# A turn more in front of TensorE's loop in an attention decode kernel on one Trainium2 core

## The chip, the cores and the metric

The kernel runs on one core of one Trainium2 chip. The metric is the device time of one execution in microseconds (us). The kernel before takes 184.91 us, the median of three runs (184.82 to 184.98).

## The reference, cut to what matters

One new token for each of 32 sequences attends to the last 512 cached positions. There are 32 query heads, and four of them share one of 8 key and value heads.

```python
B, Sq, D = x.shape                      # 32, 1, 512
Hq, Dh = 32, 128
Hkv, Sk = k_cache.shape[1], k_cache.shape[2]   # 8, 2048
W = min(4096, max(256, Sk // 4))        # 512
rep = Hq // Hkv                         # 4
q = (lambda x, *d: x.transpose(*d))((x @ wq).reshape(B, Sq, Hq, Dh), 0, 2, 1, 3)
k = jnp.repeat(k_cache[:, :, Sk - W:, :], rep, axis=1)
v = jnp.repeat(v_cache[:, :, Sk - W:, :], rep, axis=1)
scores = jnp.einsum("bhqd,bhkd->bhqk", q, k) * (Dh ** -0.5)
p = _softmax(scores, axis=-1)
o = jnp.einsum("bhqk,bhkd->bhqd", p, v)
return (lambda x, *d: x.transpose(*d))(o, 0, 2, 1, 3).reshape(B, Sq, Hq * Dh) @ wo
```

All inputs are bf16. The window of keys is 32 x 8 x 512 x 128 x 2 bytes, 33.6 MB, the values are as many, and wq and wo have 4.2 MB each.

## The kernel before

The 32 sequences are taken as eight **quads** of four, numbered 0 to 7. For one quad the keys are 4 MiB and the values 4 MiB, and each has two buffers in SBUF (`K_sb`, `V_sb`); even quads use one, odd quads the other. The buffer of wq is later a buffer of values, and that of the even keys later holds wo.

Every engine works through a list of short words, written out by hand at the top of the file (lines 20 to 37). The letter is an operation, the first number its quad:

- **T q.w** (VectorE, line 522) transposes half of the quad's keys, w being 0 or 1.
- **S q.w** (TensorE, `scores`, line 353) does half of the quad's scores, 16 matmuls.
- **M q** (VectorE, line 528) takes the row maximum, **X q** (ScalarE, line 581) the exponential with its sum, **N q** (VectorE, line 536) divides by the sum.
- **E q** (TensorE, `to_value_rows`, line 366) regroups the probabilities to the rows of the values, 16 matmuls; **G q** (ScalarE, line 588) takes them out of PSUM, and **B q.a.b** (VectorE line 542 and ScalarE line 594, heads a to b) spreads them into a block-diagonal form.
- **P q.a.b** (TensorE, `pv`, line 378) multiplies by the values, four matmuls for each step from a to b of 32.
- **C q.a.b** and **I** take the results out of PSUM, **F q** (TensorE, `fold`, line 390) folds them, **D q** (ScalarE, line 606) stores them for the output projection (line 464).

SyncE issues all large loads in one order (`LOADS`, lines 34 to 37): two halves of wq, then K0 K1 V0 K2 K3 V1 K4 V2 K5 and so on, the last values in halves, and wo in three parts W0, W1, W2. Its queue is in order. Loads of keys from K2 on wait for the second transpose of the quad two before (line 246), so K3 waits for T1.1 and K4 for T2.1; loads of values from V2 on wait for P of the quad two before (line 253). V1 overwrites wq and waits for the projection of the queries (line 250).

TensorE projects the queries first. Then come six operations written out as straight code, `PE_HEAD` (line 20): S0.0 S0.1 S1.0 S1.1 E0 E1. Then a hardware loop on TensorE alone (line 436) makes four turns; each turn does two rounds of `PE_ROUND` (line 21). Round q is S(q+2).0, P q.0.16, F(q-1), S(q+2).1, P q.16.28, E(q+2), P q.28.32. In the last turn there are no quads 8 and 9, so S, E and the second round's F stand under `pe.If(turn < NQ - 2)`. There are six such blocks in a turn. After the loop follow F6, F7 and the output projection, as straight code.

VectorE and ScalarE run straight code in the orders of lines 24 to 32. VectorE begins T0.0 T0.1 T1.0 M0 T1.1 N0 M1 N1 B0.0.4 T2.0 T2.1, and ScalarE X0 G0 X1 G1 B0.4.8 B1.4.8 X2 G2. T q.w waits for S(q-1).w, whose operand it overwrites; N1 waits for E0, which reads the same buffer `P_bf`; G and X follow their E and M. GpSimd builds the block-diagonal queries of quad q (line 316) once S(q-2).1 is done.

TensorE waits for semaphores in `awaited` (line 399 on). In the loop the value waited for is worked out in a register from the turn (`looped`, line 439), and held in a register for the rest of the turn. The semaphore for C counts both engines that take results out; a memset on GpSimd (line 295) gives it a start value of 4, so that the loop's first round, whose F stands for a quad -1, has something to find.

Of the kernel before, what the change touches and what calls it, by code (L numbers as in the profile page):

```python
# [2 lines left out]

# [13 lines left out]

PE_HEAD = "S0.0 S0.1 S1.0 S1.1 E0 E1"  # L20
PE_ROUND = "S{3}.0 P{1}.0.16 F{0} S{3}.1 P{1}.16.28 E{3} P{1}.28.32"
PE_TAIL = "F6 F7"
ROUNDS = 8
# [19 lines left out]
def ops_of(text):  # L43
    return [(w[0],) + tuple(int(n) for n in w[1:].split(".")) for w in text.split()]


def bass_standalone__sliding_block_cached__sampling_kernel(
# [7 lines left out]
):  # L55
    B, Sq, D = x.shape
    _, HKV, SK, DH = k_cache.shape
    HD = wq.shape[1]
    HQ = HD // DH
# [6 lines left out]
    NQ = B // 4  # L66
# [2 lines left out]
    NI = 32  # L69
    NG = 4  # L70

    rounds = [PE_ROUND.format(q - 1, q, q + 1, q + 2) for q in range(ROUNDS)]
    real = lambda w: int(w[1:].split(".")[0]) < NQ and w != f"F{NQ - 2}"
    rounds = [" ".join(w for w in r.split() if real(w)) for r in rounds]
    orders = {
        "PE": ops_of(" ".join([PE_HEAD] + rounds + [PE_TAIL])),
        "DVE": ops_of(DVE_OPS), "ACT": ops_of(ACT_OPS),
    }

    def counter(eng, op):  # L80

        if op[0] == "T":
            return ("DVE", "T%d" % op[2]), 1
        if op[0] == "C":
            return ("both", "C"), op[3] - op[2]
        if op[0] == "I":
            return ("both", "I%d" % op[3]), 1
        return (eng, op[0]), 1

    ends, total = {}, {("ACT", "D"): 2, ("both", "C"): 4}  # L90
    for eng, ops in orders.items():
        for op in ops:
            kind = op[0]
            key, n = counter(eng, op)
            total[key] = total.get(key, 0) + n
            if kind in "BP":
                for i in range(op[2], op[3]):
                    ends[kind, op[1], i] = key + (total[key],)
            elif kind == "C":
                for i in range(op[2], op[3]):  # L100
                    ends[kind, op[1], i] = key + (4 * op[1] + 8,)
            elif kind != "I":
                ends[op] = key + (total[key],)

# [23 lines left out]
    with ExitStack() as es:  # L128
# [14 lines left out]
        C_sb = sb("C_sb", [P, 2, 4, DH], F32)  # L143
# [52 lines left out]
        s = {n: sem(n) for n in names}  # L196
        op_sem = {key: sem("op_%s_%s" % key) for key in total}
# [20 lines left out]
        def single(eng):  # L218

            once = eng.alloc_register("once")  # L220
            eng.reg_mov(once, 1)
            return nc.Fori(0, once, 1, engines=[eng.engine], hint_back_edge=True)
# [48 lines left out]
        @block.gpsimd  # L271
        def _(pool):
            with single(pool):
                wait = Waits(pool)

                def diag(t, pattern, name):
                    pool.memset(t, 0.0).then_inc(s[name], 1)
                    pool.wait_ge(s[name], 1)
                    pool.affine_select(
                        out=t, in_=t, compare_op=ALU.not_equal, fill=1.0,  # L280
                        base=0, pattern=pattern, channel_multiplier=1,
                    ).then_inc(s[name], 1)

                diag(xsel[:, :, :], [[-1, 4], [-4, 32]], "pool_x")
                pool.memset(junk[:, 0:2], 0.0).then_inc(s["pool_j"], 1)
                pool.memset(QBD[:, :, :, :], 0.0).then_inc(s["pool_q"], 1)
                diag(F_id[:, :, :], [[-32, 4], [-1, HQ]], "pool_f")
                diag(m_id[:, :, :, :], [[-32, 4], [-4, HKV], [-1, KB]], "pool_m")
                pool.memset(F_sb[:, :, :, :], 0.0).then_inc(s["pool_fz"], 1)
                whole = [w for w in ops_of(" ".join(LOADS)) if w[0] == "V" and w[2:] == (0, R)]  # L290
                pool.memset(junk[:, 2:3], 0.0).then_inc(
                    sem_v_end[0], 16 * sum(w[1] % 2 == 0 for w in whole))
                pool.memset(junk[:, 3:4], 0.0).then_inc(
                    sem_v_end[1], 16 * sum(w[1] % 2 for w in whole))
                pool.memset(C_sb[:, 1], 0.0).then_inc(op_sem["both", "C"], 4)

                diag(E_id[:, :, :].rearrange("p e (b h) -> p e b h", b=4),
                     [[-1, REP], [-4, 4], [-16, HKV]], "pool_ei")
                pool.memset(E_sb[:, :, :, :, :], 0.0).then_inc(s["pool_e"], 1)
                pool.wait_ge(s["pool_e"], 1)  # L300
                pool.wait_ge(s["pool_ei"], 2)
                for k in range(KB):
                    pool.tensor_copy(E_sb[:, k, :, :, k], E_id[:, :, :]).then_inc(s["pool_e"], 1)
                pool.wait_ge(s["pool_e"], 5)
                pool.wait_ge(s["pool_q"], 1)
                pool.wait_ge(s["dve_QT"], 1)
                for q in range(NQ):
                    if q >= 2:
                        wait([ends["S", q - 2, 1]])
                    for b in range(4):  # L310
                        pr = slice(32 * b, 32 * b + 32)
                        if b:
                            pool.wait_ge(s["pool_qbd"], 3 * q + b)
                        elif q:
                            pool.wait_ge(s["pool_quad"], q)
                        pool.tensor_copy(  # L316
                            QBD[pr, q % 2].rearrange("p (w t) (h c) -> p w t h c", w=2, h=HKV)[
                                :, :, :, :, 4 * b:4 * b + 4],
                            QT_sb[pr, q].rearrange("p w (h e) t -> p w t h e", h=HKV),
                        ).then_inc(s["pool_quad" if b == 3 else "pool_qbd"], 1)  # L320

        @block.tensor
        def _(pe):
# [75 lines left out]
            def awaited(op):  # L399

                kind = op[0]
                if kind == "S":
                    yield op_sem["DVE", "T%d" % op[2]], 1, 1
                    if op[2] == 0:
                        yield s["pool_quad"], 1, 1
                        yield op_sem["both", "C"], 4, -4
                elif kind == "E":
                    yield op_sem["DVE", "N"], 1, 1
                elif kind == "P":
                    if op[2] == 0:  # L410
                        yield op_sem["DVE", "B"], 1, 1
                        yield op_sem["ACT", "B"], 1, 1
                        yield op_sem["ACT", "D"], 1, 1
                        yield op_sem["ACT", "G"], 1, 2
                        yield sem_v[op[1] % 2], 8, 16 - 8 * (op[1] % 2)
                    elif op[2] == 16:
                        yield sem_v_end[op[1] % 2], 8, 16 - 8 * (op[1] % 2)
                elif kind == "F" and op[1] < NQ - 1:
                    yield op_sem["both", "C"], 4, 8

            def do(op, value):
                for sm, a, b in awaited(op):
                    if (v := value(op[1], a, b)) is not None:
                        pe.wait_ge(sm, v)
                run[op[0]](*op[1:]).then_inc(op_sem["PE", op[0]], 1)
# [4 lines left out]
            pe.wait_ge(s["dve_q"], 4)  # L430
            pe.wait_ge(s["act_q"], 4)
            pe.wait_ge(s["dve_c"], 7)
            for op in ops_of(PE_HEAD):
                if op == ("E", 0):
                    pe.wait_ge(s["pool_e"], 5)
                do(op, plain)
            with nc.Fori(0, ROUNDS, 2, engines=[mybir.EngineType.PE]) as turn:
                held = {}

                def looped(q, a, b):  # L440
                    key = (skipped, a, a * q + b)
                    if key not in held:
                        v = turn * a + (a * q + b)
                        held[key] = pe.snap(v & 7 if key == (False, 1, 3) else v)
                    return held[key]

                for p in range(2):
                    words = PE_ROUND.format(p - 1, p, p + 1, p + 2).split()
                    for skipped, group in groupby(words, lambda w: w[0] in "SE" or p == 1 and w[0] == "F"):
                        with pe.If(turn < NQ - 2) if skipped else nullcontext():  # L450
                            for op in ops_of(" ".join(group)):
                                do(op, looped)
            for op in ops_of(PE_TAIL):
                do(op, plain)
# [196 lines left out]
```

## Time and profile before

| what | value |
|---|---|
| median of three runs | 184.91 us |
| the profiled execution | 184.95 us |
| its span, first to last instruction | 183.1 us |
| around the span | 1.85 us |
| TensorE busy | 118.9 us (65%), 1644 matmuls and as many weight loads |
| VectorE busy | 102.7 us (56%) |
| ScalarE busy | 53.0 us (29%) |
| GpSimd busy | 17.5 us (10%) |
| mean granted TensorE clock | 0.83 of full speed |
| read from memory | 75.53 MB, 413 GB/s over the span |
| issue to landing, keys, 4096 KB | median 22.7 us |
| issue to landing, values, 4096 KB | median 26.4 us |

The profile shows one execution. All times in it are counted from the start of the span. PE is TensorE, PEld its weight loads, DVE VectorE, ACT ScalarE, POOL GpSimd, SP SyncE; L378 is line 378 of the kernel. A load of 4096 KB at the 413 GB/s of the span takes about 10 us alone; that it lands 22.7 or 26.4 us after its issue says that others stand in the queue before it. Sixteen DMA engines share each load, and a load has landed when the last of them is done with its part.

### The profile page before, as it was taken

How to read it: one execution, taken by the hardware profiler on the slowest of the kernel's cores; microseconds unless marked ns; L12 is line 12 of the kernel's file. 1: busy time of each engine (PE TensorE's matmuls, PEld its weight loads, DVE VectorE, ACT ScalarE, POOL GpSimd, SP SyncE). 2: the span in 40 equal slices, each digit the busy share in tenths (PEclk: the TensorE clock that was granted, in tenths of full speed). 3: DMA queues.
4: the chain of work that ended last, by engine and by line, in shares of the span. 5: the costliest groups of instructions: out<-in, count | busy, mean ns of one | idle time of the engine just before them, and what ended most of it. 6: DMA issues, size and time to landing. Idle time of an engine off the chain costs nothing.

```text
span 183.1 us, 3778 instructions
## 1 busy us (share of the span) xinstructions
PE 118.9 (65%) x1644; PEld 55.4 (30%) x1644; DVE 102.7 (56%) x103; ACT 53.0 (29%) x100; POOL 17.5 (10%) x55
## 2 busy tenths in 40 slices
PE   0089204446203996896289945994599499999772
PEld 0024001003201353353035402541145154454362
DVE  0030999995339729949921895059905993503031
ACT  3000400010590015624700390028302832812041
POOL 7910050202000020020000100020000000000000
PEclk9999855555855699999859965699589999999998
DMA  6999999899999999899999999999989999999980
GB/s 219 418 465 401 451 458 444 387 429 458 454 401 401 458 454 422 383 451 454 437 401 422 458 444 408 408 458 444 444 372 444 408 451 408 444 415 437 420 363 26
DMA packets 3572, 75.63 MB, mean 413 GB/s; under 512 B 432, under 2 KB 496, under 8 KB 624
## 3 DMA queue, kind: packets, MB, share of 16 engines
q1 hardware_dynamic: 3504, 75.53, 96.6%
q8 instruction: 4, 0.07, 0.1%
q10 hardware_dynamic: 64, 0.03, 0.1%
HBM read 75.53 MB, written 0.03 MB: 413 GB/s over the span
## 4 chain that ended last, share of the span: by engine, by line
DMA 52%; PE 32%; DVE 11%; ACT 1%; SPq 1%; ACTq 1%; issue 1%; DVEq 0%
DMA V_sb<-in_v_cache_dram 26%; PE ps L378 19%; DMA K_sb<-in_wo_dram 12%; DMA K_sb<-in_k_cache_dram 11%; DVE KT_sb L522 7%; PE ps L340 4%; DMA bd<-in_x_dram 4%; PE ps L353 4%; PE ps L390 2%; PE ps L366 2%; DVE QT_sb L514 2%; DVE KT_sb L511 1%; ACT C_sb L599 1%; ACTq L200 1%; SPq L260 1%
## 5 line engine op out<-in xcount | busy, mean ns | idle before, releaser
L378 PE MATMUL ps<-V_sb,bd 32*128 32x512 bf16 x1024 | 66.9, 411 | 9.7 <-DMA V_sb<-in_v_cache_dram 9.6
L522 DVE STREAM_TRANSPOSE KT_sb<-K_sb 128x4096 f32<-128x4096 f32 x16 | 70.1, 4421 | 4.2 <-DMA K_sb<-in_k_cache_dram 4.1
L353 PE MATMUL ps<-KT_sb,QBD 128*32 128x512 bf16 x256 | 22.7, 485 | 38.3 <-DVE KT_sb L522 25.8
L378 PEld LDWEIGHTS ps<-V_sb,bd 32*128 32x128 bf16 x1024 | 27.0, 100 | 47.5 <-issue 18.6
L528 DVE TENSOR_REDUCE maxv<-ps 128x1 f32<-128x512 f32 x8 | 5.5, 687 | 30.1 <-PE ps L353 30.1
L353 PEld LDWEIGHTS ps<-KT_sb,QBD 128*32 128x32 bf16 x256 | 6.1, 107 | 50.6 <-issue 22.4
L594 ACT ACTIVATE bd<-PTc,mask 128x512 bf16<-128x512 bf16 x32 | 20.3, 710 | 0.2
L316 POOL COPY QBD<-QT_sb 32x128 bf16<-32x128 bf16 x32 | 9.2, 287 | 102.7 <-PE ps L353 86.4
L581 ACT ACTIVATE P_f<-ps,negmax 128x512 f32<-128x512 f32 x8 | 5.5, 686 | 39.0 <-DVE negmax L530 39.0
L599 ACT ACTIVATE C_sb<-ps 32x512 f32<-32x512 f32 x24 | 14.1, 587 | 5.9 <-PE ps L378 5.7
L606 ACT ACTIVATE o_sel<-ps 128x128 bf16<-128x128 f32 x8 | 2.2, 277 | 34.1 <-PE ps L390 34.1
L588 ACT ACTIVATE PTc<-ps 128x512 bf16<-128x512 f32 x8 | 4.8, 597 | 20.9 <-PE ps L366 20.9
L390 PE MATMUL ps<-C_sb,F_sb 128*128 128x128 f32 x72 | 10.6, 290 | 0.2 <-DVE C_sb L551 0.2
L366 PE MATMUL ps<-P_bf,E_sb 128*128 128x128 bf16 x128 | 9.1, 228 | 2.1 <-DVE P_bf L536 2.1
L390 PEld LDWEIGHTS ps<-C_sb,F_sb 128*128 128x128 f32 x72 | 8.8, 191 | 3.9 <-issue 3.4
L340 PE MATMUL ps<-V_sb,bd 128*128 128x512 bf16 x32 | 9.3, 462 | 0.8 <-DVE bd L490 0.8
L366 PEld LDWEIGHTS ps<-P_bf,E_sb 128*128 128x128 bf16 x128 | 7.7, 102 | 5.6 <-DVE P_bf L536 4.8
L542 DVE TENSOR_SCALAR bd<-PTc,mask 128x512 bf16<-128x512 bf16 x32 | 8.9, 343 | 0.0
L547 DVE COPY C_sb<-ps 32x512 f32<-32x512 f32 x4 | 2.8, 693 | 8.1 <-PE ps L378 8.1
L328 PE MATMUL ps<-bd 32*128 32x128 bf16 x4 | 0.6, 296 | 9.0 <-DMA bd<-in_x_dram 9.0
L511 DVE CAST KT_sb<-ps 128x512 bf16<-128x512 f32 x4 | 2.5, 684 | 6.7 <-PE ps L340 6.7
L575 ACT ACTIVATE KT_sb<-ps 128x512 bf16<-128x512 f32 x4 | 2.1, 603 | 14.3 <-PE ps L340 14.3
(34 smaller groups left out, 36.6 us busy)
## 6 DMA issues: line engine op xcount, KB each, us to landing
K_sb<-in_k_cache_dram SPq DMA_DIRECT2D x8, 4096.0 KB, 22.7
V_sb<-in_v_cache_dram SPq DMA_DIRECT2D x5, 4096.0 KB, 26.4
V_sb<-in_v_cache_dram SPq DMA_DIRECT2D x6, 2048.0 KB, 18.3
V_sb<-in_wq_dram SPq DMA_DIRECT2D x2, 2048.0 KB, 9.8
K_sb<-in_wo_dram SPq DMA_DIRECT2D x1, 2048.0 KB, 17.6
K_sb<-in_wo_dram SPq DMA_DIRECT2D x1, 1536.0 KB, 20.7
K_sb<-in_wo_dram SPq DMA_DIRECT2D x1, 512.0 KB, 21.4
out_dram<-P_bf SPq DMA_DIRECT2D x1, 32.0 KB, 1.5
```

The costliest lines, as they stand in the source:

```text
L316: pool.tensor_copy(QBD[pr, q % 2].rearrange("p (w t) (h c) -> p w t h c", w=2, h=HKV)[:, :, :, :, 4 * b:4 * b + 4], QT_sb[pr, q].rearrange ...
L340: ins = pe.matmul(ps[:, n], lhsT=xT_sb[:, kt, :], rhs=wq_sb[:, kt, n * 512:(n + 1) * 512], start=kt == 0, stop=kt == DKT - 1, tile_positio ...
L353: ins = pe.matmul(s_bank(q)[32 * c:32 * c + 32, :], lhsT=QBD[:, q % 2, 2 * w + t, c0:c0 + 32], rhs=KT_sb[:, w, :, KB * h:KB * h + KB, t], ...
L366: ins = pe.matmul(e_bank(q)[:, e * R:(e + 1) * R], lhsT=E_sb[:, k, e].rearrange("p m j -> p (m j)"), rhs=P_bf[:, k * R:(k + 1) * R], start ...
L378: ins = pe.matmul(o_banks(q)[:, b, :], lhsT=bd[pr, q % 2, 4 * g:4 * g + 4].rearrange("p r h e -> p (r h e)"), rhs=V_sb[q % 2][pr, 512 * g: ...
L390: ins = pe.matmul(f_bank(q)[:, 0:P], lhsT=F_sb[:, d].rearrange("p h d -> p (h d)"), rhs=C_sb[:, q % 2, :, 32 * d:32 * d + 32], start=d == ...
L522: return dve.transpose(KT_sb[:, w].bitcast(F32).rearrange("p r c t -> p r (c t)"), K_sb[q % 2][:, :].bitcast(F32).rearrange("p (r w c) -> ...
L528: dve.tensor_reduce(maxv[:, q:q + 1], s_bank(q), AX.X, ALU.max).then_inc(s["dve_m"], 1)
L542: ins = dve.tensor_scalar(o, i, m, None, op0=ALU.mult)
L581: return act.activation(P_f32[:, :].rearrange("p (k r) -> p k r", k=KB), s_bank(q).rearrange("p (r k) -> p k r", k=KB), ACTF.Exp, bias=neg ...
L594: ins = act.activation(o, i, ACTF.Copy, scale=m)
L599: ins = act.activation(*pick_args(q, r), ACTF.Copy)
```

## The change

`PE_HEAD` and the code that it made are gone. The loop makes five turns instead of four; the new first turn stands for rounds -2 and -1. Of these only S0.0, S0.1, E0 and S1.0, S1.1, E1 are real. So the order of the six becomes S0.0 S0.1 E0 S1.0 S1.1 E1, that of a round.

Every operation of the loop now stands under an `If`, in one of three kinds: S and E run while `turn < 8`, P and the first round's F while `late < 8`, the second round's F while `late < 6`. `late` is the turn less 2, wrapped to 14 in the first turn. There are 13 such blocks in a turn in place of six. Values waited for in the first kind are worked out from the turn, in the two others from `late`. The start value of the semaphore for C becomes 12, with all that wait for it raised by 8, so that S0.0 and S1.0 find 4 and 8. The wait for the constants of E (`pool_e`), which stood before E0, stands before the loop.

```diff
-PE_HEAD = "S0.0 S0.1 S1.0 S1.1 E0 E1"
 PE_ROUND = "S{3}.0 P{1}.0.16 F{0} S{3}.1 P{1}.16.28 E{3} P{1}.28.32"
...
-    rounds = [PE_ROUND.format(q - 1, q, q + 1, q + 2) for q in range(ROUNDS)]
-    real = lambda w: int(w[1:].split(".")[0]) < NQ and w != f"F{NQ - 2}"
+    rounds = [PE_ROUND.format(q - 1, q, q + 1, q + 2) for q in range(-2, ROUNDS)]
+    real = lambda w: -(w[0] == "F") <= int(w[1:].split(".")[0]) < NQ and w != f"F{NQ - 2}"
...
-        "PE": ops_of(" ".join([PE_HEAD] + rounds + [PE_TAIL])),
+        "PE": ops_of(" ".join(rounds + [PE_TAIL])),
...
-    ends, total = {}, {("ACT", "D"): 2, ("both", "C"): 4}
+    ends, total = {}, {("ACT", "D"): 2, ("both", "C"): 12}
...
-                    ends[kind, op[1], i] = key + (4 * op[1] + 8,)
+                    ends[kind, op[1], i] = key + (4 * op[1] + 16,)
...
-                pool.memset(C_sb[:, 1], 0.0).then_inc(op_sem["both", "C"], 4)
+                pool.memset(C_sb[:, 1], 0.0).then_inc(op_sem["both", "C"], 12)
...
-                        yield op_sem["both", "C"], 4, -4
+                        yield op_sem["both", "C"], 4, 4
...
-                    yield op_sem["both", "C"], 4, 8
+                    yield op_sem["both", "C"], 4, 16
...
-            for op in ops_of(PE_HEAD):
-                if op == ("E", 0):
-                    pe.wait_ge(s["pool_e"], 5)
-                do(op, plain)
-            with nc.Fori(0, ROUNDS, 2, engines=[mybir.EngineType.PE]) as turn:
+            pe.wait_ge(s["pool_e"], 5)
+            with nc.Fori(0, ROUNDS + 2, 2, engines=[mybir.EngineType.PE]) as turn:
+
+                late = pe.snap((turn + 14) & 15)
                 held = {}
 
-                def looped(q, a, b):
-                    key = (skipped, a, a * q + b)
-                    if key not in held:
-                        v = turn * a + (a * q + b)
-                        held[key] = pe.snap(v & 7 if key == (False, 1, 3) else v)
-                    return held[key]
+                def group_of(p, w):
+                    return "keys" if w[0] in "SE" else "fold" if p == 1 and w[0] == "F" else "values"
 
                 for p in range(2):
                     words = PE_ROUND.format(p - 1, p, p + 1, p + 2).split()
-                    for skipped, group in groupby(words, lambda w: w[0] in "SE" or p == 1 and w[0] == "F"):
-                        with pe.If(turn < NQ - 2) if skipped else nullcontext():
-                            for op in ops_of(" ".join(group)):
+                    for group, ws in groupby(words, lambda w: group_of(p, w)):
+
+                        def looped(q, a, b):
+                            key = (group, a, a * q + b)
+                            if key not in held:
+                                if group == "keys":
+                                    v = turn * a + (a * q + b - 2 * a)
+                                else:
+                                    v = late * a + (a * q + b)
+                                held[key] = pe.snap(v & 7 if key == ("values", 1, 3) else v)
+                            return held[key]
+
+                        runs = {"keys": turn < NQ, "values": late < NQ, "fold": late < NQ - 2}
+                        with pe.If(runs[group]):
+                            for op in ops_of(" ".join(ws)):
                                 do(op, looped)
```

## The prediction

> **What bounds the kernel now.** I read the page's summary first, then the chain that ended last, then the DMA records, and then the stretch around the six moved operations engine by engine.
>
> ```profile
> span 183.1 us, 3778 instructions
> ...
> DMA  6999999899999999899999999999989999999980
> ...
> q1 hardware_dynamic: 3504, 75.53, 96.6%
> q8 instruction: 4, 0.07, 0.1%
> ```
>
> The loads (queue q1) fill 96.6% of the span on all 16 DMA engines; no slice is lower than 8 tenths but the first and the last. TensorE and VectorE sit idle a third and more of it. So the kernel is a stream of 75.5 MB, and an engine's delay counts only if a load is issued so late that the stream runs dry. The chain in order of time says the same:
>
> ```profile
> 33.11 20.03 DMA K_sb<-in_k_cache_dram
> 53.15 0.02 issue
> 53.17 4.46 DVE KT_sb L522
> ...
> 158.67 21.42 DMA K_sb<-in_wo_dram
> 180.09 0.04 issue
> 180.14 0.42 PE ps L464 x15
> ```
>
> K2 lands at 53.15 and VectorE waits for it; at the end W2 lands at 180.09, and only then come the last 16 matmuls and the output.
>
> The second row of the queues is the one to look at in this change: four packets of queue q8, 65,536 bytes in all, are the program's own code. I followed the single packets of the trace. On one DMA engine a packet begins within 4 ns of the end of the one before, so the sixteen engines can be told apart. The code packets run at 47.5, 68.4, 77.8 and 85.5 us, each on one engine for 1.02 to 1.09 us; that engine's loads stand still meanwhile (holes of 1.00 to 1.07 us), and its next packet takes 1.69 to 1.76 us in place of 1.21. Together about 1.5 us. None runs after 86 us. At the end, from 176 us in 40 slices of 0.175 us:
>
> ```profile
> DMA  9839699899431222231100000000000000150000
> ```
>
> Most engines are done at 178, and a quarter or an eighth is busy until 179.5. By the packets, twelve deliver their last data at 177.8 to 178.2 us, and four at 179.24, 179.29, 179.62 and 179.64: those are the four that fetched code. As W2 has landed only when all 16 are done, **the code packets set the end of the stream**.
>
> Now the six operations, TensorE and VectorE:
>
> ```profile
> 33.14 1.90 PE L353 MATMUL ps<-KT_sb,QBD 128*32 128x512 bf16 x16 [2.23 <-DVE KT_sb L522]
> 37.47 1.90 PE L353 MATMUL ps<-KT_sb,QBD 128*32 128x512 bf16 x16 [2.43 <-DVE KT_sb L522]
> 42.58 1.90 PE L353 MATMUL ps<-KT_sb,QBD 128*32 128x512 bf16 x16 [3.22 <-DVE KT_sb L522]
> 44.41 1.58 PE L366 MATMUL ps<-P_bf,E_sb 128*128 128x128 bf16 x16
> 48.07 1.13 PE L366 MATMUL ps<-P_bf,E_sb 128*128 128x128 bf16 x16 [2.08 <-DVE P_bf L536]
> 57.75 1.90 PE L353 MATMUL ps<-KT_sb,QBD 128*32 128x512 bf16 x16 [8.55 <-DVE KT_sb L522]
> ```
>
> ```profile
> 42.61 0.48 DVE L536 TENSOR_SCALAR P_bf<-P_f,recip 128x512 bf16<-128x512 f32 x1
> 44.53 0.69 DVE L528 TENSOR_REDUCE maxv<-ps 128x1 f32<-128x512 f32 x1 [1.44 <-PE ps L353]
> 47.93 1.14 DVE L542 TENSOR_SCALAR bd<-PTc,mask 128x512 bf16<-128x512 bf16 x4
> 53.17 8.77 DVE L522 STREAM_TRANSPOSE KT_sb<-K_sb 128x4096 f32<-128x4096 f32 x2 [4.10 <-DMA K_sb<-in_k_cache_dram]
> ```
>
> These are S0.1, S1.0, S1.1, E0, E1, S2.0; and N0, M1, B0.0.4, T2.0. The last line has the cover: 4.10 us in which VectorE waits for K2.
>
> **The change part by part.**
>
> *The order.* E0 now stands ahead of S1.0, and waits for N0, which ends at 42.61 + 0.48 = 43.09. Behind it on TensorE wait S1.0 and S1.1, whose operands are ready at 37.4 and 42.5. E0 takes 1.58 us, S1.0 and S1.1 1.90 each: 43.1 + 5.4 = 48.5. M1 begins there in place of 44.53, **4.0 us later**. X1 no longer stands behind G0, so M1's begin to N1's end is what later rounds show (66.80 to 69.22, 2.42 us): N1 ends at 51.0, B0.0.4 at 52.1. T2.0 can't begin before K2 is there at 53.17. So VectorE's 4.10 us of idle time shrink to about 1.0, and T2.0, T2.1 and the issue of K4 stay. ScalarE: E1 51.1 to 52.7, G1 0.6, four spreads 2.6 (half of 4.99 for eight), so B0.4.8 is there at 55.9; P0 wants it at 59.58. GpSimd's queries for quad 3 follow S1.1 at 49.9 (four copies, 1.33), wanted by S3.0 at 73.9. Price 0.
>
> *If that cover is gone*, the stream's backlog stands behind it. When K4 is issued at 61.97, 28,672 KB have been issued (wq, K0 to K3, V0, V1), 29.36 MB. Moved by then: 18 us at 428 GB/s, 20 at 419, 20 at 443 and 2 at 419, 25.8 MB. The rest of 3.6 MB lasts 8.6 us. A load's first packet comes 1.0 us after its issue (0.73 to 1.76 at the start), so K4 may come 7.5 us later without a gap, and M1's chain 8.5 us.
>
> *The blocks under `If`*, 13 in place of 6 a turn, and a fourth way back to the loop's head. The nearest row is where P5.28.32 and P6.0.16 follow each other across a way back and a skipped block:
>
> ```profile
> 155.90 4.77 PE L378 MATMUL ps<-V_sb,bd 32*128 32x512 bf16 x80
> ...
> 161.69 3.63 PE L378 MATMUL ps<-V_sb,bd 32*128 32x512 bf16 x64
> ```
>
> The 64 matmuls of P6.16.32 take 3.63 us with a skipped block among them, so 80 would take 4.54: 0.23 us for the way back with its skipped block, 0 for the other. Bounds 0 to 0.23 for each; I take 0, as the row with a block alone has it. At 0.23 the eight blocks of the first turn between E0 and E1 cost 1.8 us, inside the 8.5. In later rounds P waits 2.0 to 3.6 us for its values (quads 2 to 4), and seven more blocks a turn at 0.23 are 0.8 us a round. At the end the last turn's groups lie ahead of V6 and V7, for which P waits 0.20 and 1.16 us, and W2 is the later one anyway.
>
> A rule that speaks against the change stands in the Trainium skill, "Runtime: NRT & Kernel Launch", section "Instruction fetch mechanics": a taken branch to code outside the window of two blocks waits for that block to be fetched. By it each way back over the loop would fetch again. The trace disagrees for TensorE's loop here: turns after the first fetch nothing, nor do the ways back at 125 and 157 us. If the rule holds in the first turn, it is the stall of the fourth rival.
>
> *The code.* 96 of 644 pairs of weight load and matmul leave the program (from the code: 4 + 32 + 96 + 368 + 16 + 128). When the packets ran, TensorE had come to about pair 116, 266, 383 and 500: one packet for some 128 new pairs. The new program has 548, with its loop at 36 to 404, and skips through it in the first turn. So I expect **three packets instead of four**, between 30 and 55 us. The first may hold up K1, which T1.0 takes up at 33.1; by the windows' rates K1 lands near 32, and 1.5 us more make T1.0 up to 0.5 us late, inside the 1.0.
>
> What does a packet less bring? Three engines late by 1.5 us still end the stream as four do. Bounds: the ends of 179.62 and 179.64 belong to two engines that without a packet would have been among the later of the twelve, those of 179.24 and 179.29 to two earlier ones. With three packets on the same engines as the first three, one of 179.62 stays: -0.02. If all three fall on early ones, 179.64 - 179.29 = 0.35 less; with the lateness at its spread, -0.40 to +0.07. I take -0.02, as the second and fourth packets sit on the late pair and only the fourth goes.
>
> *Other edits:* the `pool_e` wait is met at 9.7 us, when GpSimd's fourth copy for E ends, long before 29; the memset's larger count is the same instruction. Waits on register values in the first turn are as in S2.0, which begins 0.13 us after T2.0 ends. All 0.
>
> **Sum:** 184.95 + 0 + 0 - 0.02 = 184.93 for an execution like the profiled one, which lies 0.04 above the median: **184.89 us**.
>
> **The rivals.**
>
> 1. *The three packets fall on early engines.* W2 lands 0.33 to 0.40 us sooner: 184.91 - 0.33 = 184.58, to 184.51. For it: which engine gets which packet is not in the profile. Against: two of four sat on late ones.
> 2. *No code packet in the stream's way*, if all code is there before the loads fill the queue. The twelve other engines end at 178.2, but then TensorE bounds: from 177.22 the output matmuls need 1.08 + 0.85 + 0.43, ending at 179.6 in place of 180.57. 184.91 - 1.0 = 183.9. Against it: new code is first walked at 29 us or later, and the stream is full from 2 us on.
> 3. *Slower: two code packets on one DMA engine.* Its place is the one engine, its price 1.5 us: that engine ends at 181.1, W2 lands there, 186.4 us. It decides as soon as any engine serves two, because the spots moved, or because the jumps make code be fetched again (five turns of it must share 16 engines). Against: four packets took four engines, and no later turn fetched.
> 4. *Stalls of the skipping first turn outlast the cover.* A missed block costs a start of 1.0, a packet of 1.2 ahead of it and 1.1: 3.3 us. E1 waits for N1, S1.1 and E1 lie up to two blocks behind E0: 6.6 + 1.8 for the blocks = 8.4, still inside 8.5. A third miss ends 3.2 us late: 188.1; a part of one gives 185.3 to 185.8. Against: packets are fetched one ahead, as the one at 47.5, before E1's 48.07, shows.
>
> The change doing less than it says is no case: the straight code does go.
>
> **How the numbers follow.** Forecast 0.56, rival 1 0.18, rival 2 0.06, rival 3 0.14, rival 4 0.06. A measurement of this kernel can tell about 0.2% (0.37 us) from no change: faster is below 184.54, slower above 185.28. Rival 1 lies at that edge, half each. Faster 0.06 + 0.09 = 0.15; slower 0.14 + 0.05 = 0.19; same 0.66. The range is 184.4 to 185.8: it holds the forecast, rival 1 and the lesser part of rival 4, and leaves out rivals 2 and 3.
>
> **What would show it.** E0 begins near 43.1 and ahead of S1.0; M1 near 48.6; VectorE's wait for K2 is near 1 us and T2.0 still near 53.2; K4 is issued near 62. Queue q8 has three packets, all before 55 us. Three engines end 1.2 to 1.6 us behind the others, and W2 lands at 179.7 to 180.1. I am wrong if the instruction row shows four or more, if the stream has a slice below 8 tenths between 3 and 177 us, or if W2 lands after 180.5.

## The result, and the profile after

The changed kernel takes 185.23 us, the median of 20 runs (184.77 to 186.55), beside 184.91 for the kernel before (20 runs, 184.61 to 186.17). The ratio is 1.0027 with a 95% interval of 1.0014 to 1.004: slower by a little, where no change was forecast.

The execution that was profiled took 186.39 us with a span of 183.4. From its page, the summary, the slices of the DMA engines and the queues:

```profile
span 183.4 us, 3852 instructions
...
DMA  6998999899998999999998999899999999999980
...
q1 hardware_dynamic: 3504, 75.53, 96.4%
q8 instruction: 3, 0.05, 0.1%
```

The stream of loads is as full as before, and three code packets run inside the span in place of four. But 186.39 less 183.4 is 3.0 us around the span, where the kernel before has 1.85. The time went there, behind the last instruction. The DMA view from 176 us on, in slices of 0.35 us, shows what is there:

```profile
DMA  9499941121000000003000000001000000000000
...
q8 instruction: 1, 0.02, 0.4%
```

The "3" near 182.5 us is the store of the output. The "1" near 185.7 is a **fourth code packet**, more than 2 us behind the end of the span; by its record it runs from 185.67 to 186.62. Before has nothing there.

The span itself is 0.3 us longer in this execution. TensorE had a lower clock in rounds 4 and 5 and became the last engine. The change is not needed for that: a second profiled execution of the same kernel (span 183.0) does not have it in round 5, and one of the kernel before with padding, an experiment below, does. The stretch 148.4 to 153.2 us of these three in that order, with its length, busy times and counts of the engines, granted clock (PEclk, the third figure from the end), DMA share and GB/s:

```profile
148.40:153.20 4.80, 4.80 (x69) 1.90 (x65) 3.52 (x5) 1.06 (x2) 0.00 (x0) 0.75 1.01 430
```

```profile
148.40:153.20 4.80, 4.80 (x80) 2.48 (x76) 3.08 (x7) 0.41 (x2) 0.00 (x0) 1.00 1.00 427
```

```profile
148.40:153.20 4.80, 4.80 (x67) 2.00 (x64) 3.23 (x5) 0.76 (x2) 0.00 (x0) 0.81 0.99 420
```

From 131 to 138 us, in round 4, the granted clock of the three is 0.56, 0.80 and 0.60.

Over many runs of each, all taken beside the kernel before, time and span come apart like this (late: time less span above 1.95 us):

| kernel | runs | median us | mean us | mean span | mean time less span | late | above 2.2 |
|---|---|---|---|---|---|---|---|
| before | 140 | 184.92 | 185.06 | 183.10 | 1.96 | 34 | 13 |
| changed | 44 | 185.23 | 185.46 | 183.25 | 2.21 | 23 | 15 |
| changed, straight end | 35 | 184.88 | 184.87 | 183.04 | 1.83 | 0 | 0 |
| changed, no hint | 12 | 184.96 | 184.95 | 183.13 | 1.82 | 0 | 0 |
| before, straight end | 12 | 184.99 | 184.98 | 183.11 | 1.87 | 0 | 0 |

Of the 0.40 us between the means of the first two rows, 0.25 lie around the span and 0.15 in it. Spans are recorded to 0.1 us, so the time less span of a single run is known to 0.05 us. The rows below the first two are experiments of the next section.

There are long spans too: 9 of the 140 runs of the kernel before and 5 of the 44 of the changed one have a span of 183.8 us or more, with at most 1.87 us around it. None of the 59 runs in the three rows below has one.

The six moved operations, on TensorE and on VectorE in the profile of the changed kernel:

```profile
32.86 1.90 PE L352 MATMUL ps<-KT_sb,QBD 128*32 128x512 bf16 x16 [2.34 <-DVE KT_sb L528]
42.87 1.89 PE L365 MATMUL ps<-P_bf,E_sb 128*128 128x128 bf16 x16 [8.11 <-DVE P_bf L542]
44.69 3.60 PE L352 MATMUL ps<-KT_sb,QBD 128*32 128x512 bf16 x32
50.81 1.07 PE L365 MATMUL ps<-P_bf,E_sb 128*128 128x128 bf16 x16 [2.52 <-DVE P_bf L542]
57.98 1.90 PE L352 MATMUL ps<-KT_sb,QBD 128*32 128x512 bf16 x16 [6.10 <-DVE KT_sb L528]
```

```profile
42.33 0.49 DVE L542 TENSOR_SCALAR P_bf<-P_f,recip 128x512 bf16<-128x512 f32 x1
48.35 0.69 DVE L534 TENSOR_REDUCE maxv<-ps 128x1 f32<-128x512 f32 x1 [5.53 <-PE ps L352]
50.67 1.14 DVE L548 TENSOR_SCALAR bd<-PTc,mask 128x512 bf16<-128x512 bf16 x4
53.40 8.77 DVE L528 STREAM_TRANSPOSE KT_sb<-K_sb 128x4096 f32<-128x4096 f32 x2 [1.59 <-DMA K_sb<-in_k_cache_dram]
```

These are S0.1, E0, S1.0 with S1.1, E1, S2.0; and N0, M1, B0.0.4, T2.0. The 5.53 us before M1 are the wait for scores that now come behind E0; the 1.59 us before T2.0 are what is left of the 4.10. T2.0 begins 0.23 us later than before.

### The profile page after: what moved, and what is told of

It is laid out like the page before. It is cut to its first block, busy times and chain, and to the rows that moved or that the text cites. A ratio compares the mean times of both kernels' runs of the same rounds, so it can differ in the third digit from the quotient of the medians.

```text
span 183.4 us, 3852 instructions
## 1 busy us (share of the span) xinstructions
PE 119.4 (65%) x1644; PEld 55.6 (30%) x1644; DVE 102.6 (56%) x103; ACT 53.2 (29%) x100; POOL 17.5 (10%) x55
## 4 chain that ended last, share of the span: by engine, by line
PE 43%; DMA 41%; DVE 12%; ACT 1%; issue 1%; ACTq 1%; DVEq 0%
PE ps L377 27%; DMA V_sb<-in_v_cache_dram 26%; DMA K_sb<-in_k_cache_dram 11%; DVE KT_sb L528 7%; PE ps L339 4%; PE ps L352 4%; DMA bd<-in_x_dram 4%; PE ps L389 3%; PE ps L365 2%; DVE QT_sb L520 2%; DVE KT_sb L517 1%; ACT C_sb L605 1%; PE ps L470 1%; DVE C_sb L557 1%; ACTq L199 1%
## 5 line engine op out<-in xcount | busy, mean ns | idle before, releaser
L377 PE MATMUL ps<-V_sb,bd 32*128 32x512 bf16 x1024 | 68.3, 419 | 9.9 <-DMA V_sb<-in_v_cache_dram 9.5
L352 PE MATMUL ps<-KT_sb,QBD 128*32 128x512 bf16 x256 | 22.1, 480 | 30.2 <-DVE KT_sb L528 17.7
```

The costliest lines, as they stand in the source:

```text
L352: ins = pe.matmul(s_bank(q)[32 * c:32 * c + 32, :], lhsT=QBD[:, q % 2, 2 * w + t, c0:c0 + 32], rhs=KT_sb[:, w, :, KB * h:KB * h + KB, t], ...
L377: ins = pe.matmul(o_banks(q)[:, b, :], lhsT=bd[pr, q % 2, 4 * g:4 * g + 4].rearrange("p r h e -> p (r h e)"), rhs=V_sb[q % 2][pr, 512 * g: ...
```

## The experiments

The theory after the result: **the last packet of code is fetched too late**, and whatever TensorE still has to do behind the kernel's last instruction waits for it. The rivals: the new order, and the blocks under `If` with the fourth way back.

**The same kernel again.**

> The changed kernel once more, beside the kernel before on the same chip. Its profiled execution took 186.39 us with a span of 183.4: 3.0 us lie outside the span, where the kernel before has 1.85, and a fourth code packet runs at 185.67, behind the span's end. Late packet theory: the kernel is 1.002 to 1.004 of before, its spans stay within 0.1 of 183.1 to 183.3, and the difference of time and span varies from 1.8 to 3.3 us, with the fourth packet behind the end. Order theory and theory of the If blocks: the difference of time and span is 1.85 throughout and the spans themselves are some 0.3 us longer.

Median 185.21 of 12 runs, ratio 1.0013 (0.9988 to 1.0039). The profiled execution took 185.37 us with a span of 183.0; 7 of 12 runs were late, up to 3.39 us. Its packet is there again, from 184.73 to 185.60 us. In both profiles the packet's end lies 0.23 us behind the time of the run (186.62 beside 186.39, 185.60 beside 185.37), though one run took 1.02 us longer than the other: the end of the run moves with the end of the packet. Its start keeps no such distance; it lies 0.72 us ahead of the time of the run in one and 0.64 in the other.

**The end of the code put where it was, with the change kept.** For all padded kernels the number alone differs.

```diff
+            gate = pe.alloc_register("gate")
+            pe.reg_mov(gate, 1)
+            with pe.If(pe.snap(gate) < 1):
+                for i in range(89):
+                    pe.matmul(Y_ps[:, 0:P], lhsT=xT_sb[:, 0, :], rhs=xT_sb[:, 1, :],
+                              start=True, stop=True, tile_position=(0, 0))
             pe.wait_ge(s["dve_q"], 4)
```

> The changed kernel with 89 matmuls (178 instructions) that are jumped over ahead of the loop, so that its output projection and its end stand at the same place of the code as in the kernel before (1333 instructions in place of 1152; before has 1334). Nothing else of the change is undone. Late packet theory: four code packets, all inside the span, time less span back to 1.85 us, time 184.9 us, ratio 0.999 to 1.001. Order theory and theory of the If blocks: still 185.2 us, ratio 1.002 to 1.004.

185.01 us, ratio 1.0005 (0.9985 to 1.0025). Four packets inside the span, at 19.8, 33.1, 50.1 and 56.1 us; time less span 1.79 to 1.97, mean 1.88. Three runs are at 1.96 or 1.97, none above 2.2. Around the span that is as the late packet theory has it, and the order and all blocks under `If` were still there. The ratio by itself does not decide: its interval reaches the 1.002 of the other theories.

**The kernel before, padded to the changed kernel's place.**

```diff
+                for i in range(35):
```

> The kernel before with 35 matmuls (70 instructions) that are jumped over ahead of its straight code: 1407 instructions, 255 more than the changed kernel, so its end stands at the same place of a block of 256 as there. It has nothing of the change. Late packet theory: four code packets inside the span and a fifth behind its end, time less span 1.8 to 3.3 us, ratio 1.002 to 1.004. The two other theories: 184.9 us, ratio 1.000, with time less span at 1.85.

184.89 us, ratio 0.9998 (0.9978 to 1.0019), no late run of 11. **A miss.** There was a fifth packet, but at 181.5 us, inside the span. It has a cost of its own: in that profile the store of the output took 2.5 us to land where the kernel before has 1.5, and the span was 183.9. By the packets, the code ran from 181.49 to 182.46 us, and two pieces of the store land behind it, at 182.56 and 182.68, the others by 182.19.

```profile
out_dram<-P_bf SPq DMA_DIRECT2D x1, 32.0 KB, 2.5
```

Three of the 11 runs have a long span (183.9, 184.0 and 184.0 us), and the profiled run is the first of them. So a packet at the kernel's end can cost time inside the span as well as behind it. Whether it makes the long spans of the kernel before and of the changed kernel too is not shown, as none of those was profiled.

**The order alone.**

```diff
-PE_HEAD = "S0.0 S0.1 S1.0 S1.1 E0 E1"
+PE_HEAD = "S0.0 S0.1 E0 S1.0 S1.1 E1"
```

> The kernel before with its straight code in the order S0.0 S0.1 E0 S1.0 S1.1 E1, the loop as it was. Late packet theory: 184.9 us, ratio 1.000, M1 near 48.4 us and T2.0 still near 53.2. Order theory: 185.2 us, ratio 1.002 to 1.004.

184.91 us, ratio 1.0002 (0.9979 to 1.0026). M1 begins at 48.80, and T2.0 where it did:

```profile
53.16 8.77 DVE L522 STREAM_TRANSPOSE KT_sb<-K_sb 128x4096 f32<-128x4096 f32 x2 [0.89 <-DMA K_sb<-in_k_cache_dram]
```

The order theory falls by the trace: M1 comes 4.3 us later, and T2.0 does not. The interval by itself would still hold the 1.002 of that theory.

**Why the packet is late: the loop at the end.** The output projection is a loop of one turn whose way back carries a branch hint (line 217 on). That loop made straight:

```diff
-            with single(pe):
+            with nullcontext():
```

> The changed kernel with the output projection as straight code instead of a loop of one turn with a branch hint: 1148 instructions in place of 1152. If the hint at the loop's branch keeps the next code from being fetched ahead, the fourth packet now runs before the span's end, near 181 us, and time less span falls from 1.8 to 3.4 us to 1.85 throughout, time 184.9. If it is the place of the end alone, nothing changes: fourth packet at 184.5 to 186, time less span above 1.95 in half of the runs, time 185.2.

184.83 us, ratio 0.9994 (0.9986 to 1.0003), 11 runs between 184.67 and 184.97, none late. The fourth packet runs at 179.5 us, as the same view from 176 us on shows: it hides among the last loads, and nothing follows the store.

```profile
DMA  9599932112000000030000000000000000000000
...
q8 instruction: 1, 0.02, 0.4%
```

**Three more places of the end.** Padded as above, with 32, 64 and 126.

> The changed kernel with 32 matmuls (64 instructions) jumped over ahead of the loop, 1219 instructions. If a packet is asked for when a fixed place of the code is passed, and that place is just behind the output projection in the changed kernel, 64 instructions more bring it to the projection: fourth packet near 181 to 182 us, inside the span, time less span 1.85, time 184.9. If what counts is that the loop begins within the code that is there at the start, nothing changes: 185.2.

185.12 us, ratio 1.0027 (1.0008 to 1.0046). The packet runs at 179.1 us and no run is late (1.78 to 1.86), as the fixed place has it; but the spans are 183.1 to 184.9, mean 183.6. The last matmuls of the output show why:

```profile
180.25 0.43 PE L476 MATMUL ps<-K_sb,o_sel 128*32 128x128 bf16 x15 [0.36 <-DMA K_sb<-in_wo_dram]
181.43 0.22 PE L476 MATMUL ps<-K_sb,o_sel 128*32 128x128 bf16 x1 [0.75 <-issue]
```

The sixteenth matmul waits 0.75 us for nothing that the profile shows. I take it that it waits for its code. Then the new block begins here with the very last matmul, five instructions before the end of 1219; the unpadded kernel with its 1152 instructions ends **62 before it**. With blocks of 256 instructions (128 pairs of weight load and matmul, the prediction's reading of the packets), the kernel before with its 1334 ends 136 before the next.

> The same with 64 matmuls (128 instructions), 1283 in all. By the fixed place: fourth packet at 176 to 181 us, time less span 1.85, time 184.9. By the loop's beginning, now at about instruction 210 in place of 82 and still within the first 256: 185.2.

184.97 us, ratio 1.0004 (0.999 to 1.0017). The fourth packet came at 57.1 us, earlier than expected. Five of 12 runs were late, the highest 2.26. So the fixed place had the time right and the packet and the late runs wrong.

> The same with 126 matmuls (252 instructions), 1407 in all, as many as the padded kernel before, whose fifth packet ran at 181.5 us inside the span with time less span at 1.8. By the fixed place, one packet of 256 instructions on: five packets, the last at 181 to 186 us, and time less span as in one of the two, 1.85 or half of the runs above 1.95. By the loop's beginning, now past 256: 1.85 and 184.9 us.

184.9 us, ratio 1.0016 (0.9998 to 1.0034). Four packets, not five, in the profile of a run that was not late; four of 12 late, three of them at 2.94 to 3.02. So it is not the loop's beginning, which lies past 256 here.

**The hint alone.** The loop of one turn kept, its hint taken off for TensorE.

```diff
-        def single(eng):
+        def single(eng, hint=True):
...
-            return nc.Fori(0, once, 1, engines=[eng.engine], hint_back_edge=True)
+            return nc.Fori(0, once, 1, engines=[eng.engine], hint_back_edge=hint)
...
-            with single(pe):
+            with single(pe, hint=False):
```

> The changed kernel with the loop of one turn round the output projection kept, but without its branch hint: one instruction less, 1151. Hint theory: as with the straight end, fourth packet near 179.5 us, time less span at most 1.95, time 184.8 to 184.9. If the loop's own branch at its end is to blame and not the hint: fourth packet at 184.5 to 186, half of the runs with time less span above 1.95, 185.2.

184.96 us, ratio 0.999 (0.9972 to 1.0007); packet at 178.9 us, time less span 1.78 to 1.87 in all 12. It is the hint, not the loop. The three profiles of the changed kernel have the hint as an instruction of TensorE just ahead of the output projection, at 178.7, 177.0 and 177.1 us: about the time at which, without it, the packet is fetched.

**The straight end in the kernel before**, the same edit there.

> The kernel before with the same straight end, 1330 instructions. In 15 of 70 runs the kernel before too has time less span above 1.95. Hint theory: those go, the highest time less span is 1.95, and a packet may run near 180 us; median 184.85. If they come from something else: still one run in five above 1.95, median 184.9.

184.99 us, ratio 0.9992 (0.998 to 1.0005). None late, highest 1.94, and a fifth packet appears at 179.9 us that the kernel before does not have in its span. So the kernel before had the fault too, less often: late in 34 of 140 runs with the hint and in none of these 12.

**The straight end twice more, and the changed kernel a third time.**

> The changed kernel with the straight end once more, for its time against before: 184.83 as the first time, all runs below 185.0, ratio 0.9986 to 1.0003, if the late packet is all that separated the changed kernel from before.

184.88 us, ratio 0.9992 (0.9979 to 1.0005), packet at 178.1, none late. Four of the 12 runs lie above 185.0, up to 185.16, where none was expected.

> The changed kernel a third time, for more runs and a third profile. If its profiled run is one with time less span near 1.85, it has no packet behind the span's end, and if it is one above 2.1, a packet ends about 0.2 us behind the time of the run, as in the two profiles so far (186.62 beside 186.39, 185.60 beside 185.37). Half of the runs above 1.95, median 185.2.

185.26 us, ratio 1.0022 (0.9997 to 1.0048), 6 of 12 late. The profiled run took 184.97 with a span of 183.2, and there is no fourth packet in it at all. In a run that is not late, none is waited for.

**Does the distance to the next block decide how often?**

> The padded kernel before again (1407 instructions). Theory that the distance from the code's end to the next block of code decides (about 62 instructions here and in the changed kernel, 135 in before): the first time was an accident of its early packet at 181.5 us, and now a third of the runs or more have time less span above 2.2. If the main loop of the changed kernel decides and not the end: again none above 1.95, and a packet near 181.5.

184.85 us, ratio 0.9994 (0.997 to 1.0019). Two of 12 late, 2.51 and 3.33, and no fifth packet in the profile of one that was not. Late runs do occur, but neither theory's number came.

> The changed kernel with 16 matmuls (32 instructions) jumped over ahead of the loop: 1187 instructions, its end 27 before the next block in place of 62. Distance theory: at least as many late runs as the changed kernel, a third or more above 2.2, highest 2.9 or more. If distance has no part: about the share of before, one in ten above 2.2.

185.04 us, ratio 0.9996 (0.9972 to 1.002). Five of 12 late, four above 2.2; in the profile the packet runs from 185.52 to 186.54 and the run took 186.31, again 0.23 less. The late runs are as the distance theory has them.

> The changed kernel with 120 matmuls (240 instructions) jumped over: 1395 instructions, its end about 75 before the next block. Distance theory: between the changed kernel (62) and before (135), so two to four of 12 runs above 2.2. If distance has no part: one or none.

185.15 us, ratio 1.001 (0.9985 to 1.0036). Eight of 12 late, three above 2.2, as the distance theory has it. Its profiled run took 184.79, and its packet came from 184.05 to 184.97: just in time.

> The changed kernel with the straight end a third time, for its time against before: median 184.85 to 184.95, none with time less span above 1.95; in the mean some 0.1% below before, whose late runs it lacks.

184.9 us, ratio 0.999 (0.9969 to 1.001), packet at 177.9, none late.

With the changed kernel's loop, an end 27 to 75 instructions before the next block (unpadded, 16, 120, 126) gave 25 of 80 runs above 2.2 us, and one 136 to 187 before it (89, 64) gave 1 of 24. In the kernel before, about 62 gave 2 of 23 and 136 gave 13 of 140 (with the order alone, also 136, 1 of 12). So the distance fits the first set and not the second.

## Why the prediction was wrong

- **The order: right.** M1 was put at 48.5 us and began at 48.35; N1's end at 51.0, it was 50.76; VectorE's rest of idle time at 1.0, it was 1.59. E0 took 1.89 and not 1.58, the two halves of S1 together 3.60 and not 3.80. Price 0, as the run of the order alone shows by itself.
- **The code packets in the stream: right.** Three of them, at 33.2, 47.7 and 54.9 us. Three DMA engines deliver their last data at 179.46 to 179.60, the thirteen others at 177.84 to 178.04. So three end the stream as four do, and a packet less brings nothing. In each later profile as many engines are late as packets ran before 90 us.
- **The blocks under `If`: mis-sized, and not what made the kernel slower.** The place is that between P5.28.32 and P6.0.16. The 0.23 us of the prediction were a difference of two rows; 0 was taken for what the change adds. The idle time itself stands in the chain where TensorE is last, for the kernel before in the padded one:

```profile
159.62 0.09 issue
159.71 3.63 PE ps L378 x64
```

  In the changed kernel the chain has

```profile
159.91 0.47 issue
160.38 3.63 PE ps L377 x64
```

  and the other two profiles of it have 0.46 and 0.42. So the change adds 0.3 to 0.4 us here. In the second profile P7 still waits 1.26 us for its values behind it. It is in the end of the span only where TensorE is last, as in the first profile. The changed kernel with the straight end has the same 0.47 in its first profile, a run of 184.86 us.
- **The step that failed** is "So I expect **three packets instead of four**", and with it the sum "184.95 + 0 + 0 - 0.02 = 184.93", which carried the 1.85 us around the span over as if nothing in the change could reach them. In two of three profiles the fourth packet was not saved: in the kernel before it runs in the loop, at 85.5 us, and in the changed kernel behind the end, where it is waited for. In the third, of a run that was not late, there are three as expected. The 1.85 us around the span became 2.21 in the mean of 44 runs, where before has 1.96. The 0.15 us more in the span go with the hint too: its mean is 183.25 us, and 183.04 with the straight end.
- **The rivals.** None of the four was it. The third and the fourth looked for a packet too many and for a stall in the first turn; both were sought inside the span.

Shown by the runs: the hint keeps the last block of code from being fetched in time; without it neither kernel had a late run, 0 of 59, and the packet appears at 178 to 180 us in all five profiles; and in the three profiles of late runs the end of the run moves with the packet. Without the hint the change costs nothing that the runs can tell: with straight ends the means are 184.87 us for the changed kernel and 184.98 for the kernel before. Argued only: that what waits is code put behind the kernel. The trace ends before it. The Trainium skill, "Runtime: NRT & Kernel Launch", section "Terms", speaks of such a postamble of barriers and semaphore resets around a kernel; no run here shows its instructions. The Trainium skill, "Runtime: NRT & Kernel Launch", section "Instruction fetch mechanics", says that the next block is fetched while the present one runs, with the cost mostly hidden; at the kernel's end the runs agree without the hint and disagree with it.

Open: why only about half of the changed kernel's runs are late and the others need no packet; what asks for the packet of a late run, 1.7 to 2.3 us behind the span's end; and why the kernel before, with the same hint, is late in a quarter (34 of 140). The distance of the code's end from the next block fits the changed kernel with its padded versions, and not the kernel before with its own.

Does a version beat both? The changed kernel with the straight end is faster than the changed kernel by 0.3% (mean 184.87 against 185.46). Against the kernel before its three ratios of 0.9994, 0.9992 and 0.999 all have intervals that reach 1; in the median they are level (184.88 and 184.92), and what it gains is the late runs, 0.19 us in the mean (185.06 less 184.87).

## What to carry to other kernels

Compare an execution's time with its span before anything else: a change of the code's length can cost time behind the last instruction, which no engine's row shows. When code is taken away, see which fetch of code it removes and where the last one now falls, and look again at branch hints that were set for another length. In a kernel that loads without a pause, a fetch of code delays one DMA engine, and the last transfer waits for it, as much for three late engines as for four in these profiles.

## What was not expected of the hardware

- A hint for a branch that is not taken cost up to 1.5 us behind the end (time less span 3.39 beside 1.85), in half of the runs and not in the others.
- A code packet at 181.5 us, beside the output's store, made that store land in 2.5 us in place of 1.5.
- With 32 matmuls of padding, the very last matmul of the output projection came 0.75 us late and the end with it, though the last code packet had run from 179.1 to 180.0 us, 1.4 us before. That it waited for its code is inferred from the place of the block, not shown.
